# Unscaled k, a later third pair, and one-product maxima in the attention stage of a fused attention and expert kernel

## The chip, the cores and the metric

One core of a Trainium2 chip runs the whole program in one launch. The metric is the device time of one execution in microseconds (us). TensorE (PE) multiplies matrices into PSUM, VectorE (DVE) and ScalarE (ACT) read PSUM and SBUF, GpSimd (POOL) works on SBUF, SyncE (SP) issues the DMAs. Each engine takes its instructions in the order in which the program holds them, and waits on semaphores for the others.

## The reference

```python
def sm_attn(qq, kk, vv):                       # on q, k, v averaged over 4 neighbours
    s = scale * np.matmul(qq, kk.transpose(0, 1, 3, 2))
    a = np.exp(s - np.max(s, axis=-1, keepdims=True))
    a = a / (np.sum(a, axis=-1, keepdims=True) + 1e-09)
    return np.matmul(a, vv)
...
mask = np.abs(pos[:, None] - pos[None, :]) < factor        # factor = 4
scores = np.where(mask, scale * np.matmul(q, k.transpose(0, 1, 3, 2)), -1000000000.0)
...
return (out_up + out_local).astype(np.float32)  # pooled attention plus local attention

x = attention as [1152, 512]
x = (silu(x @ w_gate) * (x @ w_val)) @ w_out     # 512 -> 1536 -> 512
out = sum over 8 experts of P[:, e:e+1] * (relu(x @ w1[e]) @ w2[e])   # 512 -> 1024 -> 512
```

Shapes: q, k, v are (2, 8, 576, 64); `scale` is 1/8. P comes from a softmax of logits and 8 rounds of normalising rows and columns.

## The kernel before

The attention is worked in eight pairs of heads (pair 0 to 7; pairs 0 to 3 are the first batch). For each pair p these steps follow one another:

- `pooled` (L375): ACT multiplies k by -0.125 in place (L380), DVE sums q and k over four neighbours into `qd` and `kd` (L382, L383), ACT scales `kd` by 1/16 (L384). The two sums of pairs 2 and up are ordered behind the reciprocals of the pair before (`summed`).
- `scores` (L394): into three PSUM banks PE writes the mask (L399) and the local scores of five windows each (L402, banks 0 and 1), and the pooled scores (L405, bank 2). As k carries a minus sign, DVE takes minima: one reduction for each bank (L409 twice, L411), into the tile `stm`. ACT then does 13 exponentials with `scale=-1` and the minimum as bias (L417 ten times, L421 three times), each with a sum. DVE adds the sums (L425) and takes reciprocals (L426), POOL multiplies the exponentials by them (L428, L430).
- `turn` (L434): PE transposes the exponentials (L441, L445), ACT copies the result to SBUF as `at` (L447 to L450).
- `combine` (L453): PE multiplies with v (L463, L472), ACT and DVE form `x` (L475, L481), and `split` (L168, L169) makes an fp16 pair `xhl` of it.

`pooled_v` (L386) sums v over four neighbours on POOL. The banks of scores, transposes and outputs come from one ring of six (`bank`, tag `att`), so the scores of pair p+1 need banks that the exponentials of pair p still read. `attention` starts the scores of two pairs (`AHEAD`), then goes through turn(p), start(p+2), combine(p). `keep_warm` puts products of zeros into PE's queue for pairs 0 to 3, and `NWARM` such products stand at the very start.

Among this run the first steps of the next stage. For each of 12 slices f of `w_gate` and `w_val`: a load of float64 words (`load_gv`), the making of float32 from them on ACT and DVE (`from_f64`, L200 to L204: one ACT instruction and four of DVE), the maximum (L226 on ACT, then `allmax` over the partitions), and the fp16 split (`prep_gv`). `allmax` with `short` turns the column of maxima by a product (L159), reduces it (L160), and spreads the result by a second product (L161), which the users read from PSUM. The tile for this comes from `psg`, a ring of two banks that `keep_warm`, `vv` and the first products also use. `gv_step` then multiplies: 24 products of 512 columns for each f of batch 0, and 48 of 320 for each f of batch 1, which needs `xhl` of pairs 4 to 7. Slices 0, 1 and 2 of batch 0 are multiplied among pairs 4 to 7 (`EARLY`).

A scheduler that runs a model of the engines' times sets each engine's order within these rules (`gate` and `issue_after` add some).

Of the kernel before, what the change touches and what calls it, by code (L numbers as in the profile page):

```python
# [7 lines left out]
F32 = mybir.dt.float32  # L8
# [10 lines left out]
FAC, SD = 4, 144  # L19
# [9 lines left out]
WS = 64  # L29
WSTART = (0, 57, 114, 171, 228, 284, 341, 398, 455, 512)  # L30
WCUT = (0, 60, 117, 174, 231, 288, 344, 401, 458, 515, 576)
NW = 5
HQ = 48
# [16 lines left out]
UB = 8  # L50
KB = 5
HB = 4
NWARM = 5
NKEEP = 2
NQ = 3
V4B = 4
# [8 lines left out]
def tile_kernel(ctx, tc, qT, kT, vw, vd4, wgv, wo, wg2, w1, w2, out):  # L65
# [15 lines left out]
    def tmp(n, nm):  # L81
        return wp.tile([P, 16], F32, tag="tmp", bufs=56, name=nm)[:, :n]
# [15 lines left out]
    for n in range(32, P, 32):  # L98
# [7 lines left out]
    identb = ap.tile([P, P], BF16, tag="identb", bufs=1, name="identb")  # L106
    V.tensor_scalar(identb, dist, 0.0, None, op0=ALU.is_equal)
    maskb = ap.tile([P, NW, WS], BF16, tag="maskb", bufs=1, name="maskb")
    V.tensor_scalar(maskb, near[:, None, :].to_broadcast([P, NW, WS]), (2 * FAC - 1.0) ** 2, FAR,
                    op0=ALU.is_ge, op1=ALU.mult)  # L110
    ident = cp.tile([P, P], F32, name="ident")
    built.append(V.tensor_scalar(ident, dist, 0.0, None, op0=ALU.is_equal))
# [1 line left out]
    vdz = [ap.tile([HS, 2, P], F32, tag=f"vdz{i}", bufs=1, name=f"vdz{i}") for i in range(2)]  # L114
    stm = [ap.tile([P, 16], F32, tag=f"stm{i}", bufs=1, name=f"stm{i}") for i in range(2)]
    sts = [ap.tile([P, 16, 2], F32, tag=f"sts{i}", bufs=1, name=f"sts{i}") for i in range(2)]
    for i in range(2):
        V.memset(stm[i], 0.0)
        V.memset(sts[i][:, :, 0], 1.0)
        V.memset(sts[i][:, :, 1], 1e-9)  # L120
# [26 lines left out]
    def allmax(mx, n, nm, short=False):  # L147

        if n > 1:
            m = tmp(1, f"gm_{nm}")  # L150
            V.tensor_reduce(m, mx, axis=AX.X, op=ALU.max)  # L151
            mx = m
        if not short:
            g = tmp(1, f"g_{nm}")
            G.partition_all_reduce(g, mx, channels=P, reduce_op=RED.max)  # L155
            return g
        ps = psg.tile([P, 512], F32, tag="y", name=f"sm_{nm}")
        r = tmp(1, f"gr_{nm}")
        T.matmul(ps[:1, :P], lhsT=mx, rhs=ident, start=True, stop=True)  # L159
        V.tensor_reduce(r[:1], ps[:1, :P], axis=AX.X, op=ALU.max)  # L160
        T.matmul(ps[:, P:P + 1], lhsT=ones[:1], rhs=r[:1], start=True, stop=True)  # L161
        return ps[:, P:P + 1]

    def split(hi, lo, src, s, pool=False):
        if pool:
# [43 lines left out]
    def gate(after):  # L209
        return tc.issue_after(after.ins) if after else nullcontext()  # L210
# [156 lines left out]
    def attention():  # L367
# [7 lines left out]
        def pooled(pr):  # L375
            q, k = ld[pr]
            qd[pr] = ap.tile([P, SD, 2], F32, tag="qd", name=f"qd{pr}")
            kd[pr] = ap.tile([P, SD], F32, tag="kd", name=f"kd{pr}")
            with gate(exped.get(pr - 1) if pr > 1 else None):
                A.activation(k, k, AF.Copy, scale=-0.125)  # L380
            with gate(summed.get(pr - 1) if pr > 1 else None):
                V.tensor_reduce(kd[pr], k.rearrange("p (s a) -> p s a", a=FAC), axis=AX.X, op=ALU.add)  # L382
                V.tensor_reduce(qd[pr], q.rearrange("p (s a) j -> p s j a", a=FAC), axis=AX.X, op=ALU.add)  # L383
            A.activation(kd[pr], kd[pr], AF.Copy, scale=1.0 / (FAC * FAC))  # L384

        def pooled_v(pr):  # L386
            v4, vd = v4s[pr], vdz[pr % 2]
            vt = ap.tile([HS, 2, 2, P], F32, tag="vt", bufs=1, name=f"vt{pr}")
            with gate(scaled.get(pr - 1)):
                G.tensor_tensor(vt[:, 0], v4[:, :, 0], v4[:, :, 1], op=ALU.add)  # L390
                G.tensor_tensor(vt[:, 1], v4[:, :, 2], v4[:, :, 3], op=ALU.add)
                G.tensor_tensor(vd, vt[:, 0], vt[:, 1], op=ALU.add)

        def scores(pr):  # L394
            q, k = ld[pr]
            nm = f"{pr}"
            ps = bank(f"s{nm}", 3)
            for i in range(2):
                T.matmul(ps[i][:, :NW * WS], lhsT=identb, rhs=maskb.rearrange("p u w -> p (u w)"), start=True, stop=False)  # L399
                for c in range(NW):  # L400
                    ws = slice(WSTART[i * NW + c], WSTART[i * NW + c] + WS)
                    T.matmul(ps[i][:, c * WS:(c + 1) * WS], lhsT=q[:, ws].rearrange("p s j -> p (s j)"), rhs=k[:, ws],  # L402
                             start=False, stop=c == NW - 1)
            for t in range(NQB):
                T.matmul(ps[2][:2 * HQ, t * SD:(t + 1) * SD], lhsT=qd[pr][:, t * HQ:(t + 1) * HQ].rearrange("p s j -> p (s j)"),  # L405
                         rhs=kd[pr], start=True, stop=True)
            mx, sm = stm[pr % 2], sts[pr % 2]
            for i in range(2):
                V.tensor_reduce(mx[:, i:2 * NW:2], ps[i][:, :NW * WS].rearrange("p (u w) -> p u w", u=NW),  # L409
                                axis=AX.X, op=ALU.min)  # L410
            V.tensor_reduce(mx[:2 * HQ, 2 * NW:2 * NW + NQB], ps[2][:2 * HQ, :DW].rearrange("p (u w) -> p u w", u=NQB),  # L411
                            axis=AX.X, op=ALU.min)
            ex = ap.tile([P, DO + DW], F32, tag="ex", bufs=3, name=f"ex{nm}")
            for i in range(2):
                for c in range(NW):
                    w = 2 * c + i
                    A.activation(ex[:, w * WS:(w + 1) * WS], ps[i][:, c * WS:(c + 1) * WS], AF.Exp, scale=-1.0,  # L417
                                 bias=mx[:, w:w + 1], accum_out=sm[:, w, 0:1])
            for t in range(NQB):
                w = 2 * NW + t  # L420
                e = A.activation(ex[:2 * HQ, DO + t * SD:DO + (t + 1) * SD], ps[2][:2 * HQ, t * SD:(t + 1) * SD], AF.Exp,  # L421
                                 scale=-1.0, bias=mx[:2 * HQ, w:w + 1], accum_out=sm[:2 * HQ, w, 0:1])
            exped[pr] = e
            rs = ap.tile([P, 16], F32, tag="rs", name=f"rs{nm}")
            V.tensor_reduce(rs, sm, axis=AX.X, op=ALU.add)  # L425
            summed[pr] = V.reciprocal(rs, rs)  # L426
            x = ex[:, :DO].rearrange("p (w k) -> p w k", k=WS)
            G.tensor_tensor(x, x, rs[:, :2 * NW, None].to_broadcast([P, 2 * NW, WS]), op=ALU.mult)  # L428
            x = ex[:2 * HQ, DO:].rearrange("p (t k) -> p t k", t=NQB)
            scaled[pr] = G.tensor_tensor(x, x, rs[:2 * HQ, 2 * NW:2 * NW + NQB, None].to_broadcast([2 * HQ, NQB, SD]),  # L430
                                         op=ALU.mult)
            exs[pr] = ex

        def turn(pr):  # L434
            ex = exs[pr]
            nm = f"{pr}"
            pt = bank(f"t{nm}", 3)
            at = ap.tile([P, DO + 4 * SD], F32, tag="at", bufs=2, name=f"at{nm}")
            for c in range(NW):
                i, o = divmod(c * P, 512)  # L440
                T.transpose(pt[i][:, o:o + P], ex[:, c * P:(c + 1) * P], ident)  # L441
            for c in range(2):
                for t in range(NQB):
                    o = (1 - c) * P + t * 2 * HQ
                    turned[0] = T.transpose(pt[1 + c][:HS, o:o + 2 * HQ],  # L445
                                            ex[:2 * HQ, DO + t * SD + c * HS:DO + t * SD + (c + 1) * HS], ident[:2 * HQ, :2 * HQ])
            A.copy(at[:, :512], pt[0])  # L447
            A.copy(at[:, 512:DO], pt[1][:, :P])
            A.copy(at[:HS, DO:DO + 2 * SD], pt[1][:HS, P:P + 2 * SD])
            A.copy(at[:HS, DO + 2 * SD:], pt[2][:HS, :2 * SD])  # L450
            ats[pr] = at

        def combine(pr):  # L453
# [41 lines left out]
        def start(pr):  # L495
            if pr < NP:
                with tc.issue_after(built[0].ins), tc.issue_after(built[1].ins):
                    pooled(pr)
                scores(pr)
                if pr + NQ < NP:  # L500
                    load_pair(pr + NQ)

        for pr in range(AHEAD):
            start(pr)
            if pr == 0:
                pooled_v(0)
# [372 lines left out]
```

## Time and profile before

| | |
|---|---|
| time, median of 3 runs | 1024.42 us (1024.08 to 1025.7) |
| the profiled execution | 1024.88 us, span 1023.1 us |
| PE busy | 1006.8 us (98%) |
| DVE busy | 743.1 us (73%) |
| ACT busy | 444.5 us (43%) |
| POOL busy | 56.9 us (6%) |

The profiled execution's own time is 1.8 us above its span and 0.46 us above the median. Busy shares of the whole span are means over stages: the attention fills the first tenth of it. A busy PE may still be a slow or a half fed PE, since the ends of products are modelled; so the rows of single stretches are read below.

### The profile page before, as it was taken

The page shows a single profiled execution, that of the slowest core. Times are in us where ns is not written, and L with a number is a line of the kernel's source. Part 1 is how long each engine was busy: PE and PEld are TensorE (multiplying, and loading weights), DVE is VectorE, ACT ScalarE, POOL GpSimd, SP SyncE. Part 2 cuts the span into 40 slices and gives each one's busy share as a digit, 9 for nine tenths or more (in the row PEclk, how much of TensorE's full clock was granted, in tenths as well). Part 3 has the DMA queues.
Part 4 walks back from the last instruction along what each step waited for, and adds up shares of the span by engine and source line. Part 5 has one row for each costly group of instructions (what it writes and reads, how often), then busy time and mean ns, then how long its engine had stood idle before and what let it go on. Part 6 is the DMA issues. An engine that isn't in the chain of part 4 may idle for free.

```text
span 1023.1 us, 16441 instructions
## 1 busy us (share of the span) xinstructions
PE 1006.8 (98%) x6639; PEld 634.3 (62%) x6641; DVE 743.1 (73%) x1516; ACT 444.5 (43%) x926; POOL 56.9 (6%) x78
## 2 busy tenths in 40 slices
PE   8989999999999999999999999999999999999998
PEld 7765566565668657566566655756665575565644
DVE  5888788865937998797497669849757873974721
ACT  7986566665425555253235125314413521541300
POOL 4541000000001100000000000000000000000000
PEclk9989999999989999999999999999999999999999
DMA  9922143320010212121003012110301211020011
GB/s 291 277 102 97 42 165 128 121 83 1 21 63 1 84 52 73 42 81 44 5 38 122 3 42 83 43 33 9 125 1 42 83 42 42 1 83 1 1 42 52
DMA packets 12988, 67.92 MB, mean 66 GB/s; under 512 B 1584, under 2 KB 1840, under 8 KB 6512
## 3 DMA queue, kind: packets, MB, share of 16 engines
q1 hardware_dynamic: 12912, 66.87, 18.9%
q8 instruction: 52, 0.85, 0.3%
q14 instruction: 24, 0.20, 0.1%
HBM read 64.50 MB, written 2.36 MB: 65 GB/s over the span
## 4 chain that ended last, share of the span: by engine, by line
PE 77%; DVE 11%; ACT 6%; DMA 4%; issue 1%; SPq 0%; POOL 0%; ACTq 0%; DVEq 0%
PE y L176 34%; PE p L176 28%; PE gv L176 7%; PE wo L176 4%; DVE w L169 2%; DMA r<-in_w 2%; ACT ex L417 1%; DMA rawo<-in_wo 1%; DVE mxw L145 1%; DMA q<-in_qT 1%; DVE h L748 1%; PE s L402 1%; PE lgps L603 1%; DMA rawg<-in_wgv 1%; DVE cvg L203 1%
## 5 line engine op out<-in xcount | busy, mean ns | idle before, releaser
L176 PE MATMUL y<-w,hhl 128*128 128x512 f16 (+1 forms) x1752 | 396.2, 376 | 0.0
L176 PE MATMUL p<-bop,w 128*128 128x320 f16 (+1 forms) x2688 | 354.4, 286 | 1.7 <-DVE h L748 1.0
L176 PEld LDWEIGHTS <-w 128*128 128x128 f16 x2688 | 263.0, 98 | 91.8 <-issue 2.5
L176 PEld LDWEIGHTS <-hhl 128*128 128x128 f16 x1752 | 171.4, 98 | 178.2
L776 ACT ACTIVATE hhl<-h 128x640 f16<-128x640 f32 (+1 forms) x128 | 82.7, 676 | 161.6 <-DVE h L748 161.6
L176 PE MATMUL gv<-xhl,gv 128*128 128x320 f16 (+1 forms) x864 | 144.1, 328 | 1.9 <-DVE mv L357 0.8
L168 ACT ACTIVATE w<-r,s_w 128x256 f16<-128x256 f32 (+1 forms) x96 | 71.1, 783 | 117.4 <-PE y L176 86.3
L176 PEld LDWEIGHTS <-gv 128*128 128x128 f16 x864 | 84.6, 98 | 59.0 <-issue 5.6
L807 DVE SCALAR_TENSOR_TENSOR acc<-y,pe,acc 128x512 f32<-128x512 f32 (+1 forms) x64 | 47.3, 739 | 101.3 <-PE y L176 100.5
L777 DVE SCALAR_TENSOR_TENSOR hhl<-h,hhl 128x640 f16<-128x640 f32 (+1 forms) x128 | 94.1, 754 | 17.5 <-ACT hhl L776 16.6
L748 DVE SCALAR_TENSOR_TENSOR h<-p,u 128x256 f32<-128x256 f32 (+1 forms) x192 | 84.7, 453 | 15.7 <-PE p L176 9.8
L169 DVE SCALAR_TENSOR_TENSOR w<-r,s_w,w 128x256 f16<-128x256 f32 (+1 forms) x96 | 78.2, 833 | 16.8 <-ACT w L168 16.7
L176 PE MATMUL wo<-ahl,wo 128*128 128x320 f16 (+1 forms) x432 | 73.9, 333 | 0.0
L168 ACT ACTIVATE w<-cmb,s_w 128x512 f16<-128x512 f32 x64 | 43.0, 710 | 42.1 <-DVE cmb L280 40.0
L176 PEld LDWEIGHTS <-wo 128*128 128x128 f16 x432 | 43.3, 101 | 28.2
L748 DVE SCALAR_TENSOR_TENSOR u<-p,u 128x320 f32<-128x320 f32 (+1 forms) x128 | 57.4, 449 | 3.6 <-PE p L176 3.2
L765 ACT ACTIVATE s<-p 128x256 f32<-128x256 f32 (+1 forms) x64 | 25.4, 397 | 55.7 <-PE p L176 55.5
L145 DVE TENSOR_REDUCE mxw<-r 128x1 f32<-128x1024 f32 x32 | 37.4, 1213 | 16.3 <-DMA r<-in_w 16.1
L169 DVE SCALAR_TENSOR_TENSOR w<-cmb,s_w,w 128x512 f16<-128x512 f32 x64 | 46.1, 742 | 0.1
L300 ACT ACTIVATE j<-r 128x1024 f16<-128x1024 f32 x32 | 33.4, 1046 | 26.6 <-DMA r<-in_w 26.6
L155 POOL PARTITION_ALL_REDUCE g_w<-gm_w x16 | 6.3, 394 | 595.1 <-DVE gm_w L151 589.2
L748 DVE SCALAR_TENSOR_TENSOR u<-p,s 128x256 f32<-128x256 f32 (+1 forms) x64 | 28.8, 451 | 5.1 <-PE p L176 4.3
(192 smaller groups left out, 824.8 us busy)
## 6 DMA issues: line engine op xcount, KB each, us to landing
r<-in_w SPq DMA_DIRECT2D x32, 1024.0 KB, 4.8
rawg<-in_wgv SPq DMA_DIRECT2D x12, 1024.0 KB, 5.1
rawo<-in_wo SPq DMA_DIRECT2D x6, 1024.0 KB, 5.9
q<-in_qT SPq DMA_DIRECT2D x8, 576.0 KB, 6.9
vz<-in_vw SPq DMA_DIRECT2D x8, 320.0 KB, 6.7
k<-in_kT SPq DMA_DIRECT2D x8, 288.0 KB, 6.8
v<-in_vd SPq DMA_DIRECT2D x8, 288.0 KB
out<-acc SPq DMA_DIRECT2D x8, 256.0 KB, 2.0
```

The costliest lines, as they stand in the source:

```text
L145: V.tensor_reduce(o, i, axis=axis, op=ALU.max, apply_absolute_value=True)
L168: return (A.activation(hi, src, AF.Copy, scale=s), V.scalar_tensor_tensor(lo, src, s, hi, op0=ALU.mult, op1=ALU.subtract))
L169: V.scalar_tensor_tensor(lo, src, s, hi, op0=ALU.mult, op1=ALU.subtract))
L176: T.matmul(ps, lhsT=wf(i, k), rhs=xf(j, k), start=n == 0, stop=n == 3 * nk - 1)
L203: V.scalar_tensor_tensor(o, hi, 0xC0000000, o, op0=ALU.bitwise_and, op1=ALU.bitwise_or)
L300: A.activation(junk, t[:, 2 * j:2 * j + 2].rearrange("p a n -> p (a n)"), AF.Abs, accum_out=mx[:, 2 * i + j:2 * i + j + 1])
L402: T.matmul(ps[i][:, c * WS:(c + 1) * WS], lhsT=q[:, ws].rearrange("p s j -> p (s j)"), rhs=k[:, ws], start=False, stop=c == NW - 1)
L748: V.scalar_tensor_tensor(o, ps, HSC, u, op0=ALU.mult, op1=ALU.add)
L765: A.activation(s1, p1, AF.Copy, scale=HSC)
L776: ra = A.activation(t[:, 0], h, AF.Relu)
L777: rv = V.scalar_tensor_tensor(t[:, 1], h, 0.0, t[:, 0], op0=ALU.max, op1=ALU.subtract)
L807: V.scalar_tensor_tensor(acc[t][:, ds], ps, p[:, t:t + 1], acc[t][:, ds], op0=ALU.mult, op1=ALU.add)
```

## The change

In the diff the line numbers of before stand first. k and `kd` stay unscaled, so the scores keep their sign and lack the factor: the mask becomes negative, the reductions take maxima, a new DVE instruction multiplies the 16 columns of `stm` by a tile `fac` (-0.125 and -0.125/16), and the exponentials carry 0.125 and 0.125/16 as scale. Scores of pair 2 are started before the first turn, `pooled_v` comes behind the scaling of its own pair, the four copies of pair 0's transposes go to DVE, `allmax` with `short` does one product with the column spread over 128 as weights, and `NWARM` goes from 5 to 9.

```diff
-NWARM = 5
+NWARM = 9
...
-    V.tensor_scalar(maskb, near[:, None, :].to_broadcast([P, NW, WS]), (2 * FAC - 1.0) ** 2, FAR,
+    V.tensor_scalar(maskb, near[:, None, :].to_broadcast([P, NW, WS]), (2 * FAC - 1.0) ** 2, -FAR,
...
+    fac = ap.tile([P, 16], F32, tag="fac", bufs=1, name="fac")
+    V.memset(fac[:, :2 * NW], -0.125)
+    V.memset(fac[:, 2 * NW:], -0.125 / (FAC * FAC))
...
-        if not short:
-            g = tmp(1, f"g_{nm}")
+        g = tmp(1, f"g_{nm}")
+        if short:
+            ps = psg.tile([P, 512], F32, tag="y", name=f"sm_{nm}")[:, :P]
+            T.matmul(ps, lhsT=mx.to_broadcast([P, P]), rhs=ident, start=True, stop=True)
+            V.tensor_reduce(g, ps, axis=AX.X, op=ALU.max)
+        else:
             G.partition_all_reduce(g, mx, channels=P, reduce_op=RED.max)
-            return g
-        ps = psg.tile([P, 512], F32, tag="y", name=f"sm_{nm}")
-        r = tmp(1, f"gr_{nm}")
-        T.matmul(ps[:1, :P], lhsT=mx, rhs=ident, start=True, stop=True)
-        V.tensor_reduce(r[:1], ps[:1, :P], axis=AX.X, op=ALU.max)
-        T.matmul(ps[:, P:P + 1], lhsT=ones[:1], rhs=r[:1], start=True, stop=True)
-        return ps[:, P:P + 1]
+        return g
...
-            with gate(exped.get(pr - 1) if pr > 1 else None):
-                A.activation(k, k, AF.Copy, scale=-0.125)
...
-            A.activation(kd[pr], kd[pr], AF.Copy, scale=1.0 / (FAC * FAC))
...
-            with gate(scaled.get(pr - 1)):
+            with gate(scaled[pr]):
...
-                                axis=AX.X, op=ALU.min)
+                                axis=AX.X, op=ALU.max)
...
+            V.tensor_tensor(mx, mx, fac, op=ALU.mult)
...
-                    A.activation(ex[:, w * WS:(w + 1) * WS], ps[i][:, c * WS:(c + 1) * WS], AF.Exp, scale=-1.0,
+                    A.activation(ex[:, w * WS:(w + 1) * WS], ps[i][:, c * WS:(c + 1) * WS], AF.Exp, scale=0.125,
...
-            A.copy(at[:, :512], pt[0])
+            copy = A.copy if pr else V.tensor_copy
+            copy(at[:, :512], pt[0])
...
-        for pr in range(AHEAD):
+        for pr in range(AHEAD + 1):
...
-            start(pr + AHEAD)
+            if pr:
+                start(pr + AHEAD)
```

The order on DVE at the very start, around the first reductions of pairs 0 and 1 (`s0_1` is bank 1 of pair 0's scores, `rs` the sums and reciprocals). Before:

```order
L382 TENSOR_REDUCE kd1_211<-k1_135 128x144
L383 TENSOR_REDUCE qd1_210<-q1_137 128x288
L409 TENSOR_REDUCE stm0_111<-s0_0_156 128x5
L409 TENSOR_REDUCE stm0_111<-s0_1_157 128x5
L411 TENSOR_REDUCE stm0_111<-s0_2_158 96x3
L425 TENSOR_REDUCE rs0_191<-sts0_113 128x16
L426 RECIPROCAL rs0_191<-rs0_191 128x16
L409 TENSOR_REDUCE stm1_112<-s1_0_216 128x5
```

Now:

```order
L382 TENSOR_REDUCE qd1_216<-q1_144 128x288
L407 TENSOR_REDUCE stm0_115<-s0_1_162 128x5
L409 TENSOR_REDUCE stm0_115<-s0_2_163 96x3
L407 TENSOR_REDUCE stm1_116<-s1_0_220 128x5
L411 TENSOR_TENSOR stm0_115<-stm0_115,fac_119 128x16
L407 TENSOR_REDUCE stm1_116<-s1_1_221 128x5
L409 TENSOR_REDUCE stm1_116<-s1_2_222 96x3
L411 TENSOR_TENSOR stm1_116<-stm1_116,fac_119 128x16
```

The multiplication by `fac`, which every exponential of pair 0 reads, stands behind all three reductions of pair 0 and behind the first of pair 1.

The order on DVE ahead of the exponentials of pair 4, with the float32 words of slice 1 (`cvg1`) and the rounding tiles of slice 0 (`u_gv0`, `s_gv0`, `i_gv0`) among it. Before:

```order
L383 TENSOR_REDUCE qd4_622<-q4_258 128x288
L382 TENSOR_REDUCE kd4_623<-k4_256 128x144
L481 TENSOR_TENSOR x11_549<-o1_0_521,avd1_547 128x288
L481 TENSOR_TENSOR x11_549<-o1_1_522,avd1_547 128x224
L481 TENSOR_TENSOR tail_121<-o1_1_522,avd1_547 128x64
L409 TENSOR_REDUCE stm0_111<-s4_0_628 128x5
L169 SCALAR_TENSOR_TENSOR xhl_127<-x10_417,s_x10_383,xhl_127 128x512
L409 TENSOR_REDUCE stm0_111<-s4_1_629 128x5
L169 SCALAR_TENSOR_TENSOR xhl_127<-x11_549,s_x10_383,xhl_127 128x512
```

Now, the last rows of the same stretch:

```order
L407 TENSOR_REDUCE stm0_115<-s4_1_628 128x5
L203 TENSOR_SCALAR cvg1_582<-cvg1_582 128x1024
L142 TENSOR_SCALAR u_gv0_573<-u_gv0_573 128x1
L204 SCALAR_TENSOR_TENSOR cvg1_582<-rawg1_445,cvg1_582 128x1024
L143 TENSOR_SCALAR s_gv0_574<-u_gv0_573 128x1
L144 TENSOR_SCALAR i_gv0_575<-u_gv0_573 128x1
L409 TENSOR_REDUCE stm0_115<-s4_2_629 96x3
L205 SCALAR_TENSOR_TENSOR cvg1_582<-rawg1_445,cvg1_582 128x1024
L541 TENSOR_SCALAR iv0_0_1029<-i_gv0_575,i_x10_387 128x1
L411 TENSOR_TENSOR stm0_115<-stm0_115,fac_119 128x16
```

Before, five rows stood between the reciprocal of pair 3 and the first reduction of pair 4, after which five of its exponentials could start; now nineteen rows stand between that reciprocal and the multiplication by `fac`, which all thirteen wait for.

## Rows read from the trace of the kernel before

**Rows 1.** Windows: start:end, length, busy of PE, PEld, DVE, ACT, POOL, clock, DMA, GB/s.

```profile
40.00:60.00 20.00, 19.41 (x233) 15.53 (x231) 18.39 (x38) 18.80 (x77) 6.80 (x9) 1.00 0.65 207
70.00:80.00 10.00, 9.22 (x53) 5.19 (x53) 8.51 (x25) 6.58 (x29) 3.37 (x4) 0.50 0.00 1
82.92:98.10 15.18, 14.70 (x149) 8.31 (x148) 12.66 (x29) 10.38 (x21) 0.38 (x1) 1.00 0.36 108
```

**Rows 2.** PE's longest wait from 109 us on: sum, count, mean.

```profile
PE lgps L603 <- ACT x L618: 1.5, 1, 1.5
```

**Rows 3.** Timeline of the start: start, duration, engine, line, operation, tiles, [idle before].

```profile
1.17 2.31 PE L90 MATMUL pw<-warm 128*128 128x512 bf16 x5 [1.17 <-DVE dist L93]
5.82 4.51 PE L402 MATMUL s<-k,q 128*128 128x64 f32 x20
10.76 0.31 ACT L417 ACTIVATE ex<-s,stm 128x64 f32<-128x64 f32 x1 [2.43 <-DVE stm L409]
20.99 2.44 PE L402 MATMUL s<-k,q 128*128 128x64 f32 x20 [0.87 <-ACT k L380]
```

**Rows 4.** Timeline, single places on DVE, ACT and PE.

```profile
20.14 0.25 DVE L426 RECIPROCAL rs<-rs 128x16 f32<-128x16 f32 x1
36.90 0.25 DVE L426 RECIPROCAL rs<-rs 128x16 f32<-128x16 f32 x1
38.93 0.74 DVE L481 TENSOR_TENSOR x<-o,avd 128x288 f32<-128x288 f32 x2
39.60 0.21 DVE L481 TENSOR_TENSOR tail<-o,avd 128x64 f32<-128x64 f32 x1
41.92 0.35 ACT L417 ACTIVATE ex<-s,stm 128x64 f32<-128x64 f32 x1
47.54 0.24 DVE L426 RECIPROCAL rs<-rs 128x16 f32<-128x16 f32 x1
79.11 0.23 DVE L426 RECIPROCAL rs<-rs 128x16 f32<-128x16 f32 x1
108.88 3.71 PE L176 MATMUL gv<-xhl,gv 128*128 128x320 f16 x26
```

**Rows 5.** Groups of instructions, 20 to 80 us: busy, mean ns of one, idle before.

```profile
L383 DVE TENSOR_REDUCE qd<-q 128x288 f32<-128x1152 f32 x6 | 7.8, 1295 | 0.0
L409 DVE TENSOR_REDUCE stm<-s 128x5 f32<-128x320 f32 x12 | 5.7, 483 | 0.8 <-PE s L402 0.6
L203 DVE SCALAR_TENSOR_TENSOR cvg<-rawg,cvg 128x1024 uint32<-128x1024 uint32 x4 | 5.3, 1318 | 0.0
L382 DVE TENSOR_REDUCE kd<-k 128x144 f32<-128x576 f32 x6 | 4.4, 738 | 0.0
L380 ACT ACTIVATE k<-k 128x576 f32<-128x576 f32 x6 | 4.3, 718 | 0.0
L169 DVE SCALAR_TENSOR_TENSOR xhl<-x,s_x,xhl 128x512 f16<-128x512 f32 x4 | 3.9, 987 | 0.5 <-ACT xhl L168 0.5
L447 ACT COPY at<-t 128x512 f32<-128x512 f32 x6 | 3.7, 616 | 0.0
L411 DVE TENSOR_REDUCE stm<-s 96x3 f32<-96x432 f32 x6 | 3.6, 595 | 0.3 <-PE s L405 0.3
L201 DVE TENSOR_SCALAR cvg<-cvg 128x1024 f32<-128x1024 f32 x4 | 2.7, 686 | 1.8 <-ACT cvg L200 1.8
L138 DVE TENSOR_SCALAR u_gv<-sm_gv 128x1 f32<-128x1 f32 x2 | 0.3, 153 | 0.0
```

**Rows 6.** Chain of waits, steps in order of time: start, duration.

```profile
10.76 3.07 ACT ex L417 x20
13.83 1.05 ACT ex L421 x6
76.29 4.65 PE gv L176 x12
94.75 2.69 PE gv L176 x12
```

More of the change, by code (lines that the diff above doesn't have):

```diff
@@ L409, in scores @@
                 V.tensor_reduce(mx[:, i:2 * NW:2], ps[i][:, :NW * WS].rearrange("p (u w) -> p u w", u=NW),
-                                axis=AX.X, op=ALU.min)
+                                axis=AX.X, op=ALU.max)
             V.tensor_reduce(mx[:2 * HQ, 2 * NW:2 * NW + NQB], ps[2][:2 * HQ, :DW].rearrange("p (u w) -> p u w", u=NQB),
-                            axis=AX.X, op=ALU.min)
+                            axis=AX.X, op=ALU.max)
+            V.tensor_tensor(mx, mx, fac, op=ALU.mult)
             ex = ap.tile([P, DO + DW], F32, tag="ex", bufs=3, name=f"ex{nm}")
@@ L421, in scores @@
                 e = A.activation(ex[:2 * HQ, DO + t * SD:DO + (t + 1) * SD], ps[2][:2 * HQ, t * SD:(t + 1) * SD], AF.Exp,
-                                 scale=-1.0, bias=mx[:2 * HQ, w:w + 1], accum_out=sm[:2 * HQ, w, 0:1])
+                                 scale=0.125 / (FAC * FAC), bias=mx[:2 * HQ, w:w + 1], accum_out=sm[:2 * HQ, w, 0:1])
             exped[pr] = e
@@ L446, in turn @@
                                             ex[:2 * HQ, DO + t * SD + c * HS:DO + t * SD + (c + 1) * HS], ident[:2 * HQ, :2 * HQ])
-            A.copy(at[:, :512], pt[0])
-            A.copy(at[:, 512:DO], pt[1][:, :P])
-            A.copy(at[:HS, DO:DO + 2 * SD], pt[1][:HS, P:P + 2 * SD])
-            A.copy(at[:HS, DO + 2 * SD:], pt[2][:HS, :2 * SD])
+            copy = A.copy if pr else V.tensor_copy
+            copy(at[:, :512], pt[0])
+            copy(at[:, 512:DO], pt[1][:, :P])
+            copy(at[:HS, DO:DO + 2 * SD], pt[1][:HS, P:P + 2 * SD])
+            copy(at[:HS, DO + 2 * SD:], pt[2][:HS, :2 * SD])
             ats[pr] = at
```

## The prediction, made before the changed kernel ran

> **What bounds the kernel now.** I read the windows first, and stage by stage, since the mean of the whole span (PE 98%) hides the attention. In 40 to 60 us DVE is busy for 18.39 of 20 us and ACT for 18.80 [rows 1]: both are full, and they are full because each does the other work of the stage while the other one is at the softmax. PE's 19.41 us there is not work at full rate. From the first products of batch 1 on (`gv` of 320 columns, at 108.88 us [rows 4]) PE is dense: the waits for other engines have 1.5 us as their longest [rows 2]. PE's order behind that product is as good as the same in both kernels. So the question is one: when does the first 320-column product start? What comes later moves with it. It needs `xhl` of pairs 4 to 7, and these hang on a chain that I follow by the reciprocals of each pair: they start at 20.14 (pair 1), 36.90 (pair 3), 47.54 (pair 4) and 79.11 us (pair 7) [rows 4].
>
> **The change part by part.**
>
> *The barrier.* This is the part that decides. Before, the first five exponentials of a pair wait for one reduction; the others follow as the second and third reductions come. Now all 13 wait for the multiplication by `fac`, which waits for three reductions, and it stands in DVE's one queue behind whatever was put between them. The multiplication itself is small: between 0.15 us (a 128x1 step) and 0.25 us (the 128x16 reciprocal) [rows 5, 4]; I take 0.15. The reciprocal of a pair in its turn waits for all the exponentials, so DVE can't go on with the next pair. Thus a pair now costs a sum of two parts: DVE's work from a reciprocal to the next `fac`, and ACT's exponentials.
>
> Pair 4 worked out, as its order is shown above. Before, from the reciprocal at 36.90 to the first exponential at 41.92 us it took 5.0 us, and 5.6 us more to the next reciprocal [rows 4]. Now nineteen instructions stand between: three of `x1` (0.74 + 0.21), `kd` 0.74, `qd` 1.30, three reductions (2 x 0.48 + 0.60), `xhl` 0.99, two conversions of 0.69 and two of 1.32, `g_gv0` (between 0.15 and 0.60; 0.25), five small ones of 0.15 [rows 4, 5]: 10.5 us. Single instructions overlap by some 0.07 us at their borders (38.93 + 0.74 = 39.67 stands beside a next start at 39.60 [rows 4]), 1.4 us for twenty. With `fac` that is 9.3 us, and 0.9 us more for the reciprocal's own end and for a wait on ACT's conversion that precedes these: 10.2 us. Then 13 exponentials, 4.1 us (3.07 + 1.05 [rows 6]), with one conversion of slice 2 on ACT put between them (as long as L226, 1.1 us [rows 5]), and behind them on DVE the sum, three instructions of `x2`, a conversion of 1.32 and the reciprocal: 7.9 us in all. The link takes 18.1 us where it took 10.6.
>
> The other links by the same durations and the changed order. Reciprocal 1 to exponentials 2: `kd`, `qd`, the third reduction, `fac`, and the pooled scores between, 3.5; to reciprocal 2, 4.6. To exponentials 3: 9.0, since all four DVE steps that make slice 0, `x0` and `g_v0` stand in front; to reciprocal 3, 6.3 (two other ACT steps lie among the exponentials). Pair 5: 5.9 + 4.6, no conversion in front. Pair 6: 9.4 + 5.0 (`x3`, its `xhl`, slice 3). Pair 7: 8.7 + 4.6. From reciprocal 1 to reciprocal 7 that is 3.5 + 4.6 + 9.0 + 6.3 + 10.2 + 7.9 + 5.9 + 4.6 + 9.4 + 5.0 + 8.7 + 4.6 = 79.7 us, against 79.11 - 20.14 = 59.0 us before [rows 4]: 20.7 us more.
>
> *The start.* `NWARM` adds four products to five that took 2.31 us [rows 3]; they end ahead of the data of pair 0, so they cost nothing. [...] In return the exponentials of pair 0 wait for three reductions and one of pair 1: start 12.3 us instead of 10.76 [rows 6]. Pair 1 follows at 16.4, and reciprocal 1 comes to end at 21.0 where it was 20.4: 0.6 us later. Pair 2's scores ahead of the first transposes cost 2.4 us of PE's time there [rows 3], under the exponentials of pair 1.
>
> *k unscaled.* Eight multiplications of 0.72 us go from ACT [rows 5], and those of `kd`. In 40 to 60 us ACT was full [rows 1], so this would be worth something if the two engines still overlapped. As ACT now waits at each pair for `fac`, it is worth nothing on the chain: DVE sums k directly, and stands later anyway.
>
> *Four copies to DVE (pair 0).* The nearest rows are ACT's copy of 512 columns, 0.62 us, and DVE's reduction of 432 columns from PSUM, 0.60 us [rows 5]. So the four take some 1.6 to 2.0 us on either engine; on DVE they lie under the exponentials of pair 2, which run on ACT. I take 0, and 2.0 if `fac` of pair 2 were late. [...]
>
> *Pooled v behind the scaling, one-product maxima.* POOL is busy for 6.80 of 20 us [rows 1]; its queue has room, and pooled v is needed only after the copies of the same pair: 0, at most 0.5 us a pair. The maximum loses a one-column product of PE and its wait; DVE reduces 128 rows of 128 in place of one row. Between -0.3 and +0.3 us for each of some 14; I take 0, since neither is last on the chain in the early slices.
>
> *The tail.* Some of the 20.7 us is paid back. Before, 108.88 - 79.34 = 29.5 us lie between the end of reciprocal 7 and the first 320-column product [rows 4]. There PE was held up: in 70 to 80 us its granted clock was 0.50 [rows 1], twelve products of 512 columns took 4.65 us at 76.29 and 2.69 later [rows 6]. Now, as the exponentials of pair 7 are later, two of these groups of twelve have been done by then. Left for PE are, by the changed order, 60 products of 512 columns (2.69/12 = 0.224 us each [rows 6], 13.4 us) and the transposes of pair 7 and outputs of pairs 6 and 7. For these: in 82.92 to 98.10 us PE was busy for 14.70 us [rows 1] with just these and with 36 such products (8.1 us) and two small ones (some 0.8); 5.8 us remain. Reciprocal 7 ends at 21.0 + 79.7 = 100.7; 1.7 us go by until the copies of pair 6, which stand behind the exponentials of pair 7 on ACT, are done; 100.7 + 1.7 + 13.4 + 5.8 = 121.6 us. That is 12.7 us after 108.88.
>
> **Sum.** 0.6 + 20.7 - 8.6 in the tail = 12.7 us. The profiled execution took 1024.88 us (0.46 above the median of 1024.42), so 1037.6 us, rounded to 1037.5.
>
> **The rivals.** *A*, the forecast: the chain through `fac` with a warm start, 1037.5. If single links are 0.5 us off each way, its own range is 1031 to 1043.
>
> [...]
>
> *C: ScalarE was the bound (the other side).* ACT is the fuller engine [rows 1]. If DVE's conversions find room under the exponentials and `fac` comes just behind the third reduction, what decides is ACT's work, and eight multiplications of 0.72 us are gone: 1024.9 - 5.8 = 1019 us. It decides once the steps of DVE between a reciprocal and the next `fac` sum to less than the 5.0 us of before; in pair 5 they nearly do (5.9), in pairs 3, 4, 6 and 7 they are at 8.7 to 10.2. [...]
>
> *D: it cancels.* The chain slips as in A, but by some 10 us only, and PE, which has to do the same products in any case, loses none of them: 1025, within 0.2% (about 2 us, what a measurement of this kernel can tell from no change).
>
> *E:* the chain slips and half of the slip is paid back beyond the tail as well: 1029, slower but below A's range.
>
> **How the numbers follow.** A 0.52, B 0.25, C 0.11, D 0.07, E 0.05. Faster is C, 0.11; the same is D, 0.07; slower is A, B and E, 0.82. The range goes from 1026 (C and D left out, 0.18) to 1045 (B and the upper ends of its unknowns, 2 us for the copies and 0.5 us for POOL): 1026 to 1045.
>
> **What would show it.** In the trace after: the first exponential of a pair starts right behind a 128x16 multiplication on DVE (right), not behind a reduction. The reciprocals of pairs 3, 4 and 7 near 44, 62 and 100 us (A), 49, 67 and 105 (B), or at or ahead of 36.9, 47.5 and 79.1 (C). ACT idle before the exponentials, by 3 us and more in pairs 3, 4, 6 and 7 (A); PE's twenty score products of pair 0 near 2.4 us (A) or 4.5 us (B). The first product of 320 columns near 121.6 us; waits of PE behind it as short as before. I am wrong if that product comes late and the end doesn't (then PE had slack behind it), or if DVE shows that its steps overlap more than I allow.

## The result

| | before | changed |
|---|---|---|
| time, median | 1025.06 us (4 runs, 1024.08 to 1027.13) | 1039.71 us (4 runs, 1037.35 to 1043.07) |
| ratio of the times | | 1.0143, 95% interval 1.0108 to 1.0177 |
| the profiled execution, its span | 1024.88, 1023.1 us | 1038.61, 1036.8 us |
| reciprocal of pair 1, 3, 4, 7 starts | 20.14, 36.90, 47.54, 79.11 us | 19.73, 44.36, 63.31, 101.47 us |
| first product of batch 1 (320 columns) | 108.88 us | 124.3 us |

The kernel became slower by 1.4%, inside the range and on the side that was forecast. The forecast of 1037.5 us lies 1.1 us under the profiled execution and 2.2 under the median. Of the runs told below, one execution each of e7 and e12 took over 1.5% longer than the fastest of its kernel, and the ratios and medians leave both out.

The profile of the changed kernel, windows with the columns of [rows 1]. The first two windows are one link of the chain: from the reciprocal of pair 3 to the multiplication by `fac` of pair 4, and from there to the reciprocal of pair 4.

```profile
44.36:54.08 9.72, 6.43 (x84) 5.00 (x82) 9.72 (x20) 3.88 (x7) 4.56 (x5) 0.99 0.46 159
54.08:63.31 9.23, 5.76 (x24) 4.33 (x25) 5.98 (x13) 8.30 (x35) 0.00 (x0) 0.50 0.43 149
40.00:60.00 20.00, 11.78 (x111) 8.29 (x109) 13.36 (x27) 14.11 (x57) 4.56 (x5) 0.85 0.57 193
```

In the first window DVE never stops (9.72 of 9.72 us) and ACT has 3.88 us to do; in the second ACT has 8.30 of 9.23 and DVE waits in part. Over 40 to 60 us both engines fall from 18.39 and 18.80 us [rows 1] to 13.36 and 14.11: they take turns. PE, busy for 5.76 of 9.23 us, shows a granted clock of 0.50 in the second window.

The same link as a timeline (start, duration, engine, line, operation, [idle before]) on DVE and ACT, as the forecast worked it out:

```profile
44.36 0.25 DVE L425 RECIPROCAL rs<-rs 128x16 f32<-128x16 f32 x1
47.19 0.48 DVE L407 TENSOR_REDUCE stm<-s 128x5 f32<-128x320 f32 x1
...
52.31 0.60 DVE L409 TENSOR_REDUCE stm<-s 96x3 f32<-96x432 f32 x1
52.83 1.21 DVE L205 SCALAR_TENSOR_TENSOR cvg<-rawg,cvg 128x1024 uint32<-128x1024 uint32 x1
53.96 0.20 DVE L541 TENSOR_SCALAR iv<-i_gv,i_x 128x1 f32<-128x1 f32 x1
54.08 0.17 DVE L411 TENSOR_TENSOR stm<-stm,fac 128x16 f32<-128x16 f32 x1
52.37 1.15 ACT L169 ACTIVATE gv<-cvg,s_gv 128x1024 f16<-128x1024 f32 x1 [5.28 <-DVE s_gv L143]
54.13 1.06 ACT L227 ACTIVATE rawg<-cvg 128x1024 f16<-128x1024 f32 x1 [0.61 <-DVE cvg L205]
55.19 0.29 ACT L416 ACTIVATE ex<-s,stm 128x64 f32<-128x64 f32 x1
63.31 0.25 DVE L425 RECIPROCAL rs<-rs 128x16 f32<-128x16 f32 x1
```

The first reduction of pair 4 is over at 47.7 us, and in the kernel before five exponentials could have followed it. Here they start at 55.19 us, with `fac` at 54.08. ACT had stood idle for 5.28 us ahead of 52.37. The last step ahead of these exponentials is not `fac` itself but ACT's own maximum over slice 1 (L227, to 55.19 us), whose words DVE made ahead of `fac`: the conversions stand ahead of the exponentials in both queues.

The waits of DVE in 9 to 110 us (us in total, times, longest), first the kernel before, then the changed one:

```profile
DVE rs L425 <- ACT ex L421: 8.3, 5, 2.4
```

```profile
DVE rs L424 <- ACT ex L420: 15.1, 6, 4.1
```

It is the other half of the turn: DVE waits for the exponentials almost twice as long. The end of the stage, from the list of one line's instructions up to the first 320-column product (count, ns, first and last start, forms):

```profile
L177 PE MATMUL gv<-xhl,gv x97: 296/379/634, 82.4 to 124.3; 128*128 128x512 f16 x96, 128*128 128x320 f16 x1
```

As before, 96 products of 512 columns come ahead of it; it starts 15.4 us later. Behind it PE's waits are as they were (the longest again 1.5 us, as in [rows 2]), and 912.5 us follow where 914.2 followed before.

### The profile page after: what moved, and what is told of

The parts are those of the page before. It is cut to its first block, busy times and chain, and to the rows that moved or that the text cites. A ratio compares the mean times of both kernels' runs of the same rounds, so it can differ in the third digit from the quotient of the medians.

```text
span 1036.8 us, 16426 instructions
## 1 busy us (share of the span) xinstructions
PE 1008.8 (97%) x6629; PEld 636.3 (61%) x6631; DVE 748.8 (72%) x1530; ACT 437.5 (42%) x906; POOL 58.3 (6%) x78
## 4 chain that ended last, share of the span: by engine, by line
PE 82%; DVE 10%; ACT 5%; DMA 1%; issue 1%; SPq 0%; ACTq 0%; DVEq 0%
PE y L177 36%; PE p L177 31%; PE gv L177 9%; PE wo L177 4%; ACT ex L416 2%; DVE cvg L204 1%; DVE cvg L205 1%; DMA rawo<-in_wo 1%; DVE qd L382 1%; DVE w L170 1%; PE lgps L604 1%; DMA q<-in_qT 1%; ACT ex L420 1%; DVE cvg L203 1%; DVE xhl L170 1%
## 5 line engine op out<-in xcount | busy, mean ns | idle before, releaser
L778 DVE SCALAR_TENSOR_TENSOR hhl<-h,hhl 128x640 f16<-128x640 f32 (+1 forms) x128 | 94.2, 752 | 16.6 <-ACT hhl L777 15.4
L749 DVE SCALAR_TENSOR_TENSOR h<-p,u 128x256 f32<-128x256 f32 (+1 forms) x192 | 84.8, 451 | 18.4 <-PE p L177 12.7
```

The lines of the kernel that those rows point to most:

```text
L749: V.scalar_tensor_tensor(o, ps, HSC, u, op0=ALU.mult, op1=ALU.add)
L778: rv = V.scalar_tensor_tensor(t[:, 1], h, 0.0, t[:, 0], op0=ALU.max, op1=ALU.subtract)
```

## The experiments

The theory: all 13 exponentials of a pair wait for one DVE instruction, which the scheduler puts behind other DVE work; so DVE and ACT take turns. Its rivals: other parts of the change make the loss, or the wait itself costs as much wherever it stands. Each experiment stands with its ratio to the kernel before, timed beside it. In all of them a scheduler sets the order anew, so an edit moves other instructions too; where that matters it is said.

| | ratio, 95% interval | median us | reciprocal 1, 3, 7 | first 320-column product |
|---|---|---|---|---|
| changed kernel | 1.0143, 1.0108 to 1.0177 | 1039.71 | 19.7, 44.4, 101.5 | 124.3 |
| e1 barrier on before | 1.0225, 1.0188 to 1.0262 | 1048.3 | 23.3, 53.3, 110.6 | 136.8 |
| e2 fac per bank | 1.0020, 0.9999 to 1.0040 | 1027.3 | 19.1, 41.3, 89.1 | 116.5 |
| e3 conversions behind fac | 1.0036, 1.0010 to 1.0061 | 1028.43 | 19.6, 43.8, 94.7 | 115.1 |
| e4 k scaled again | 0.9994, 0.9973 to 1.0014 | 1024.73 | 17.3, 40.0, 84.8 | 109.2 |
| e5 five warm products | 1.0151, 1.0116 to 1.0186 | 1040.02 | 23.1, 47.5, 104.6 | 128.0 |
| e6 before, nine warm products | 1.0013, 0.9985 to 1.0041 | 1024.85 | 17.2, 42.9, 85.9 | 116.6 |
| e7 per bank and behind | 0.9964, 0.9944 to 0.9984 | 1020.67 | 19.0, 42.0, 89.6 | 109.1 |
| e8 k scaled and behind | 1.0022, 1.0001 to 1.0042 | 1027.87 | 17.0, 41.4, 81.3 | 113.4 |
| e9 e7 with k multiplied | 1.0065, 1.0041 to 1.0089 | 1031.51 | 18.9, 44.9, 96.3 | 121.7 |
| e10 e7, third pair late | 1.0051, 1.0033 to 1.0069 | 1030.11 | 19.3, 46.6, 97.4 | 119.2 |
| e11 e7, copies on ACT | 1.0031, 1.0015 to 1.0047 | 1028.61 | 18.7, 42.8, 90.2 | 113.2 |
| e12 e7, two-product maxima | 1.0068, 1.0039 to 1.0096 | 1031.3 | 19.6, 42.2, 86.8 | 115.3 |

**The barrier alone, on the kernel before.**

```diff
+    fac = ap.tile([P, 16], F32, tag="fac", bufs=1, name="fac")
+    V.memset(fac, 1.0)
...
+            V.tensor_tensor(mx, mx, fac, op=ALU.mult)
```

> The kernel before (k still scaled, minima), with one DVE instruction more for each pair: the 16 minima are multiplied by a tile of ones, and all 13 exponentials wait for that. It computes the same. Theory (the wait of all exponentials for one instruction behind the conversions on DVE makes the loss): the reciprocals come late as in the changed kernel, reciprocal 3 at 43 to 46 us, 4 at 62 to 66, 7 at 98 to 106 us, and the time is 1035 to 1043 us. Rival (unscaled k, the copies on DVE, or pair 2's early scores make the loss): the multiplication costs its own 0.16 us per pair, reciprocal 7 stays within 3 us of 79, and the time is 1024 to 1027 us.

It was 2.25% slower, 5 us above what the theory expected, and its reciprocals came 4 to 7 us later than the theory had them. The link of pair 4, timeline of DVE and ACT:

```profile
53.33 0.25 DVE L429 RECIPROCAL rs<-rs 128x16 f32<-128x16 f32 x1
...
62.79 0.47 DVE L411 TENSOR_REDUCE stm<-s 128x5 f32<-128x320 f32 x1
63.19 0.59 DVE L413 TENSOR_REDUCE stm<-s 96x3 f32<-96x432 f32 x1
63.99 0.69 DVE L203 TENSOR_SCALAR cvg<-cvg 128x1024 f32<-128x1024 f32 x1 [0.21 <-ACT cvg L202]
64.60 0.70 DVE L415 TENSOR_TENSOR stm<-stm,fac 128x16 f32<-128x16 f32 x1
65.42 0.32 ACT L420 ACTIVATE ex<-s,stm 128x64 f32<-128x64 f32 x1 [1.46 <-DVE stm L415]
69.85 0.25 DVE L429 RECIPROCAL rs<-rs 128x16 f32<-128x16 f32 x1
```

From reciprocal to exponentials it takes 12.1 us, with four conversions, the split of slice 0 and the first step of slice 2 ahead of the product with ones. One multiplication by 1 in each pair is enough for the whole loss. It is more than enough: the changed kernel, which has the other parts too, is 0.8% faster than e1.

**The barrier split in three.**

```diff
             for i in range(2):
-                V.tensor_reduce(mx[:, i:2 * NW:2], ...)
+                m = mx[:, i:2 * NW:2]
+                V.tensor_reduce(m, ...)
+                V.tensor_tensor(m, m, fac[:, i:2 * NW:2], op=ALU.mult)
...
-            V.tensor_tensor(mx, mx, fac, op=ALU.mult)
```

> The changed kernel, with fac multiplied bank by bank: three small DVE instructions, each right behind its reduction as far as the scheduler has it so, in place of one behind all three. Theory: the first five exponentials of a pair start again ahead of the conversions; reciprocal 7 comes at 84 to 93 us and the time falls to 1026 to 1033 us, in spite of 16 DVE instructions more. Rival (the loss lies in other parts of the change): 1037 to 1041 us, and reciprocal 7 near 101 us.

16 DVE instructions more, and 1.2% less time than the changed kernel: back within 0.2% of the kernel before, though not shown to be equal to it. Reciprocal 7 came at 89.1 us, in the middle of what was expected. In pair 4 the exponentials of the first bank start behind the first small product (45.87 us, with 45.17 for the product), and in 40 to 60 us DVE is busy for 18.90 us and ACT for 16.55, where they had 13.36 and 14.11 in the changed kernel and 18.39 and 18.80 before [rows 1]:

```profile
45.17 0.58 DVE L409 TENSOR_TENSOR stm<-stm,fac 128x5 f32<-128x5 f32 x1
45.87 0.32 ACT L417 ACTIVATE ex<-s,stm 128x64 f32<-128x64 f32 x1
40.00:60.00 20.00, 17.59 (x189) 12.93 (x189) 18.90 (x43) 16.55 (x60) 10.30 (x10) 1.00 0.62 196
```

**The barrier left, the work ahead of it moved behind.** Each slice is converted one pair later, and its DVE steps are queued behind `fac`.

```diff
-CONV = {1: (1, 2), 3: (3,), 5: (4,), 7: (5,)}
+CONV = {1: (0,), 2: (1,), 3: (2,), 4: (3,), 5: (4,), 7: (5,)}
...
-            V.tensor_tensor(mx, mx, fac, op=ALU.mult)
+            facd[pr] = V.tensor_tensor(mx, mx, fac, op=ALU.mult)
...
-            with gate(exped[3] if f == 1 else None):
-                conv_gv(f, x1_done[pr])
+            with gate(facd.get(pr + 2)):
+                conv_gv(f, exped[2] if f == 0 else x1_done[pr - 1])
```

> The changed kernel, with the four DVE steps that make slices 0 to 4 ordered behind the multiplication by fac of the next pair (they are called one pair later and queued behind it); the barrier itself stays. Theory (the price is the DVE work that stands between a reciprocal and fac, not the wait as such): the links from reciprocal to fac fall to 5 to 7 us, the conversions lie under the exponentials, reciprocal 7 comes at 80 to 88 us, and the time is 1021 to 1029 us. Rival (a wait of all 13 for one instruction costs whatever stands ahead of it): reciprocal 7 at 96 us or later and 1034 us or more.

The time fell to 1028.43 us, as the theory had it; reciprocal 7 came at 94.7, between the two expectations. The windows of the link of pair 4, reciprocal to `fac` and `fac` to reciprocal:

```profile
43.76:48.95 5.19, 5.13 (x51) 4.26 (x49) 5.19 (x12) 2.74 (x7) 4.56 (x5) 1.00 0.35 98
48.95:54.72 5.77, 3.44 (x47) 2.35 (x47) 5.47 (x13) 5.48 (x29) 0.00 (x0) 0.96 0.95 337
```

The link is 10.96 us in place of 18.95, as long as the 10.64 of the kernel before [rows 4], and in its second half DVE and ACT are both busy (5.47 and 5.48 of 5.77 us). So the wait as such is cheap; what stands ahead of it is dear. Not all links healed: the one from reciprocal 2 to reciprocal 3 kept 14.7 us, as the conversion of slice 1 on ACT stands ahead of `avd` in ACT's queue and waits for its load (slice 0 was converted at 29.75 us).

```profile
33.54 1.13 ACT L201 ACTIVATE cvg<-rawg 128x1024 f32<-128x1024 f32 x1 [2.63 <-DMA rawg<-in_wgv]
34.88 0.76 DVE L482 TENSOR_TENSOR x<-o,avd 128x288 f32<-128x288 f32 x2 [3.45 <-ACT avd L476]
```

**k scaled again, no fac.**

```diff
+            with gate(exped.get(pr - 1) if pr > 1 else None):
+                A.activation(k, k, AF.Copy, scale=-0.125)
...
+            A.activation(kd[pr], kd[pr], AF.Copy, scale=1.0 / (FAC * FAC))
...
-            V.tensor_tensor(mx, mx, fac, op=ALU.mult)
```

(with minima, a positive mask and `scale=-1.0` again)

> The changed kernel, with k scaled again on ACT, minima and no fac; the later third pair's order, pooled v, the copies, the one-product maxima and nine warm products stay. Theory: no barrier, so reciprocal 7 returns to 74 to 80 us and the time to 1020 to 1027 us. Rival (the other parts share the loss): 1031 us or more.

The time is that of the kernel before (0.9994). Of the expectation the time held and reciprocal 7 did not: it came at 84.8 us, 5.7 later than before, and still the first 320-column product starts at 109.2. So an earlier chain isn't the only thing that sets this product: PE's 96 products ahead of it must be done too.

**Five and nine warm products.**

```diff
-NWARM = 9
+NWARM = 5
```

> The changed kernel with five products of zeros at the start in place of nine; from pair 2 on DVE's order is the same. Theory (the nine products bring the higher clock for the first scores): the twenty score products of pair 0 take about 4.5 us again, reciprocal 1 comes at 22.5 to 24 us in place of 19.7, all later reciprocals slip by as much, and the time is 1040 to 1045 us. Rival (the clock would have risen without them): reciprocal 1 at 19 to 21 us and 1036 to 1040 us.

> The kernel before with nine products of zeros at the start and nothing else. Theory: reciprocal 1 at 17 to 18 us in place of 20.1, the later ones earlier by 1 to 3 us, the time 1021 to 1024 us. Rival (what the start gains is lost in the tail, where PE has its products of 512 columns to do in any case): 1024 to 1027 us.

PE's first score products in the changed kernel and, below, in the same kernel with five:

```profile
1.17 4.02 PE L90 MATMUL pw<-warm 128*128 128x512 bf16 x9 [1.17 <-DVE dist L93]
5.56 1.52 PE L400 MATMUL s<-k,q 128*128 128x64 f32 x10
7.06 1.23 PE L400 MATMUL s<-k,q 128*128 128x64 f32 x10
```

```profile
1.17 2.31 PE L90 MATMUL pw<-warm 128*128 128x512 bf16 x5 [1.17 <-DVE dist L93]
5.55 2.23 PE L400 MATMUL s<-k,q 128*128 128x64 f32 x10
7.85 2.23 PE L400 MATMUL s<-k,q 128*128 128x64 f32 x10
```

With five, ten products take 2.23 us; with nine the first ten take 1.52 and the second ten 1.23. The granted clock has a mean of 1.00 over 0 to 20 us in both, so it does not show what makes the difference. The reciprocals slip by 3.3 us at pair 1 and 3.2 at pair 7, and the first 320-column product by 3.6, as expected. The times don't show it (1.0151 and 1.0143, with intervals of 0.35% each way): the 909.9 us behind that product were 2.6 less than in the changed kernel's profile. On the kernel before, the nine products bring reciprocal 1 forward by 2.9 us and the time not at all (1.0013): the time is the rival's. That the gain is lost in the tail isn't shown: the profile belongs to one of the longer executions (1033.25 us, 8 above the median), and there reciprocal 3 is already 6 us later than before.

**Both repairs.**

> The changed kernel with both repairs: fac bank by bank, and the conversions of slices 0 to 4 behind the last of these. Theory (two parts of one loss): reciprocal 7 at 80 to 88 us, the time 1021 to 1026 us, less than with either repair alone (1027.3 and 1028.4). Rival (both repairs give back the same microseconds, or the tail eats the rest): 1026 to 1030 us.

(the edits of e2 and e3 together, with the conversions behind the last of the three products with `fac`)

1020.67 us, by the ratio 0.36% less than the kernel before, interval 0.16 to 0.56%: the time is less than with either repair alone, as the theory had it, and this version beats both kernels. Reciprocal 7 is not the reason, at 89.6 us against the 80 to 88 expected. In its profile the first 320-column product starts at 109.1 us, as in the kernel before, and the 5 us between the two profiled executions lie behind it (914.2 us there in the kernel before, 908.9 here); some three of them are told below, under the hardware.

**Which parts of the change are worth something, once the barrier is mended.** The same repair without `fac`, and then e7 with one part undone at a time.

In e8 the third reduction takes the place of `fac` in the ordering:

```diff
-            V.tensor_reduce(mx[:2 * HQ, 2 * NW:2 * NW + NQB], ...)
+            facd[pr] = V.tensor_reduce(mx[:2 * HQ, 2 * NW:2 * NW + NQB], ...)
```

> The changed kernel with k scaled again, minima and no fac, and with the conversions of slices 0 to 4 ordered behind the third reduction of the next pair. Theory: reciprocal 7 at 76 to 84 us and 1019 to 1024 us. Rival (ACT, which scales k again, is now as full as in the kernel before, so nothing is left to gain): 1024 to 1028 us.

```diff
+            with gate(exped.get(pr - 1) if pr > 1 else None):
+                A.activation(k, k, AF.Copy, scale=1.0)
...
+            A.activation(kd[pr], kd[pr], AF.Copy, scale=1.0)
```

> The kernel of e7 (fac bank by bank, conversions behind), with ACT's two multiplications per pair put back, by a factor of 1: k and kd pass through ACT as in the kernel before, and the rest computes as in e7. Theory (once DVE and ACT overlap again, ACT's 0.72 us for k in each of eight pairs stands on the path, the mechanism of the rival that was to make the change faster): 1024 to 1029 us, 4 to 7 us above e7. Rival (k's scaling hides even there): 1020 to 1023 us.

```diff
-        for pr in range(AHEAD + 1):
+        for pr in range(AHEAD):
...
-            if pr:
-                start(pr + AHEAD)
+            start(pr + AHEAD)
```

> The kernel of e7 with the scores of pair 2 behind the first turn again, as in the kernel before. In e7 PE waits 6.2 us at 15 to 21 us for qd of pair 2, with the first transposes behind that in its queue. Theory (the early third pair blocks PE's queue more than it helps): the transposes of pair 0 start near 16 us in place of 22.8, reciprocal 3 comes 1 to 3 us earlier than 42.0, and the time falls to 1017 to 1021 us. Rival (PE has slack there, and pair 2 loses its head start): reciprocal 2 comes 1 to 3 us later than 25.7 and the time is 1021 to 1025 us.

```diff
-            copy = A.copy if pr else V.tensor_copy
+            copy = A.copy
```

> The kernel of e7 with the four copies of pair 0's transposes on ACT again. Theory (the copies cost the same on either engine and lie beside a wait): no change, 1019 to 1023 us. Rival (VectorE is the slower reader of PSUM and the fuller engine): 1016 to 1019 us. Other rival (ACT is late with the exponentials of pair 2): 1023 to 1026 us.

In e12 `allmax` is again, word for word, what the minus lines of the change show.

> The kernel of e7 with the maximum over partitions made by two products again (a column turned, its maximum, a second product that spreads it). Theory (the prediction's: neither form is last on the chain): 1019 to 1024 us. Rival (the second product and its way from DVE back to PE and to DVE delay the fp16 slices, so that the products of 512 columns start later): 1024 to 1029 us.

The amounts here and below are differences of the ratios, times 1025 us, each good to some 3 us. e8's time is its rival's: 5.9 us above e7 and no better than before. e9 put the two multiplications alone back and cost 10.4 us against e7, more than the 4 to 7 expected; ACT spends 8.2 us on them (5.6 for k, 2.6 for `kd`). So the mechanism of the rival that was to make the change faster is there: k's scaling does stand on the path, once DVE and ACT overlap. PE shows one place of it, the scores of pair 2, which wait for k, as that multiplication is ordered behind the exponentials of pair 1 (in e7 these scores start at 12.4 us, and reciprocal 2 comes 2.9 us earlier):

```profile
19.26 4.53 PE L404 MATMUL s<-k,q 128*128 128x64 f32 x20 [5.32 <-ACT k L382]
```

e10's theory fell. (The title and e4's text speak of a later third pair; the change starts the scores of pair 2 earlier, and e10 puts them back.) In e7 (and in the changed kernel) PE's queue does stand for 6.16 us with the pooled scores of pair 2 at its head, and without that the transposes of pair 0 start at 16.40 us, as expected. But the time rose by 8.9 us, beyond the rival's range too, reciprocal 2 came 2.4 us later and reciprocal 3 4.6 us later: pair 2's head start is worth more than the wait. First the row of the changed kernel, then of e10:

```profile
21.99 1.72 PE L403 MATMUL s<-kd,qd 128*96 128x144 f32 x6 [6.16 <-DVE qd L382]
```

```profile
16.40 1.33 PE L442 MATMUL t<-ident,ex 128*128 128x128 f32 x5 [4.04 <-POOL ex L429]
```

e11 (6.9 us above e7) fits none of its three expectations: its time lies above them all, though what the first rival starts from is in the traces (DVE's copy of 512 columns took 0.68 us and ACT's 0.60 in the changed kernel, and DVE was busy for 20.00 us in 40 to 60 us of e7, ACT for 14.47), and ACT isn't late with pair 2 (reciprocal 2 at 25.56 us, in e7 at 25.70). Where its loss comes from is open. e12 (10.7 us above) went its rival's way, and beyond its range. Reciprocal 7 comes 2.8 us earlier than in e7 and the first 320-column product 6.2 us later. At the first group of 512 columns 5.8 of these are there already (79.66 us, in e7 73.84): the scores of pair 7 stand ahead of it, and PE's granted clock has a mean of 0.78 over 60 to 80 us (0.83 in e7). The second product of a maximum is seen to hold PE up only later, where it waits for DVE, and the group behind it takes 4.44 us for 12 products, where the groups at 85.82 and 91.78 us take 2.76; the mean granted clock is 0.93 over 80 to 100 us and 0.95 over 100 to 120 (1.00 in e7 for both). So the rival's mechanism is there, but most of the delay isn't shown to be its work:

```profile
97.30 0.38 PE L164 MATMUL sm_gv<-gr_gv,ones 1*128 1x1 f32 x2 [0.46 <-DVE gr_gv L163]
98.26 4.44 PE L179 MATMUL gv<-xhl,gv 128*128 128x512 f16 x12 [0.58 <-DVE act L568]
```

The four amounts (10.4, 8.9, 6.9 and 10.7 us) can't be added: together they are 37 us, and the kernel before, which lacks all four parts, is 4 us slower than e7. Each edit lets the scheduler set a new order, and how much of an amount is the part and how much the order was not separated.

## Why the prediction was right, and which of its terms were off

- **The barrier** is right as the cause, shown by e1 (alone, it makes the loss) and by e2 and e3 (split, or with the work behind it, most of the loss goes). Of the signs set down for it, the exponentials start within 0.15 us of the end of `fac` in pairs 0, 2, 3 and 6, and 0.5 to 0.9 us after it in pairs 4, 5 and 7, where another step stands ahead of them in ACT's queue. ACT is idle for 5.9 to 7.1 us between reciprocal and exponentials in pairs 3, 4 and 6, but for 1.8 us only in pair 7, where 3 and more were forecast.
- **The link of pair 4** was worked out as 10.2 + 7.9 us and measured 10.6 + 8.4 (reciprocal end at 44.61, exponentials at 55.19, reciprocal end at 63.56).
- **The chain** from reciprocal 1 to 7 was 79.7 us by the forecast and measured 101.47 - 19.73 = 81.7. The term most off is the link of pair 2, 3.5 us to its exponentials: it took 4.9. PE's granted clock fell to 0.50 (20 to 26 us) in its wait of 6.16 us for `qd`, and the pooled scores took 1.72 us there (0.93 in pair 0, at a clock of 1.00).
- **The start** came 1.0 us earlier than forecast (reciprocal 1 ends at 19.98, not 21.0): the exponentials of pair 0 start at 11.35 us, not 12.3. That the first scores come faster with nine products was the author's estimate, and the 0.6 us of the sum rests on it. No run shows a change of the clock behind it: in the kernel before, the granted clock is 1.00 both where twenty score products took 4.51 us (5.82 to 10.33) and where they took 2.44 (20.99 to 23.43). What the runs show is the time of the products: 1.52 and 1.23 us for the two tens of pair 0 with nine, 2.23 each with five. Rival B, by which they keep the 4.51 us of before and the time is 1042, is out.
- **The tail** was 20.9 us by the forecast and took 22.6 (124.33 - 101.72). One group of twelve 512-column products took 4.09 us at a granted clock of 0.67 (the next one 2.76 us at 1.00), which no term had, and PE waited 0.84 us more:

```profile
105.85 4.09 PE L177 MATMUL gv<-xhl,gv 128*128 128x512 f16 x12
110.60 2.76 PE L177 MATMUL gv<-xhl,gv 128*128 128x512 f16 x12
114.20 0.47 PE L463 MATMUL o<-at,vdz 72*64 72x144 f32 x4 [0.84 <-issue]
```

- **The sum**: -1.0 + 2.0 + 1.7 = 2.7 us too little up to the first 320-column product, and 1.7 us less behind it: 1038.6 where 1037.5 was forecast. Good agreement of the sum, in part by terms that cancel. Rivals D and E are out: the slip is 22.4 us at reciprocal 7, 15.4 at that product and 13.7 at the end of the profiled executions.
- **Reciprocal 7 as the measure** holds only where it is late. In the profiles that have it at 94 us or later the product follows it by 20 to 26 us; where it comes at 79 to 90 us the product starts at 108.9 to 116.6, in no order (89.6 and 109.1 in e7, 81.3 and 113.4 in e8).
- **The terms put at nothing** are where the working was weakest. e1 without them is 8.6 us slower than the changed kernel with them. Two differences are seen in the rows: the start (reciprocal 1 at 23.3 in e1, 3.6 later), whose faster score products the forecast did count, and the link of pair 2 (reciprocal 1 to 2 takes 13.2 us in e1 and 9.5 in the changed kernel), which fits the early third pair, charged with PE's time only. What unscaled k is worth beside an undivided `fac` was put at nothing too, and no run shows it alone. The sum held since it was made from the changed order, where the early pair's link is short, and not by adding parts to the old chain.
- **The four copies**: the one of 512 columns took 0.68 us on DVE where ACT takes 0.60:

```profile
24.64 0.68 DVE L447 COPY at<-t 128x512 f32<-128x512 f32 x1
45.11 0.60 ACT L447 COPY at<-t 128x512 f32<-128x512 f32 x1
```

  Yet e11, which has these copies on ACT, was slower than e7: the 0.08 us are not what decides there.
- **Rival C** had the right mechanism and the wrong condition. By e9 ACT's scaling of k does cost once the engines overlap; in the changed kernel they don't. Its point of decision, DVE's work between a reciprocal and `fac` against 5.0 us, fits: with 5.2 us in e3's link that link was as short as before. An exponential with a scale of 0.125 starts 0.29 us behind the one before it (55.19, then 55.48 us), as with the scale of -1 before (41.92, then 42.21 us).

## What to carry to other kernels

An instruction that gathers several results before the next engine may start costs more than its own time: it can cost all that a scheduler or an order puts ahead of it on its engine (here `fac` took 0.17 us in pair 4, and the link 18.95 us in place of 10.64). Where one engine's saving puts such a join into the loop of two engines that are both full, split the join along the parts that the other engine takes, and queue movable work behind it; here only the version with both was faster than the kernel before. To price such a change, walk the two engines' new order link by link; a price for each part, added to the old chain, would have missed here by some 8 us (e1 against the changed kernel).

## What the runs showed of the hardware

PE waits once for 1.5 us near 285 us, in the kernel before [rows 2] as in e7 (and at 301 us in the changed one). In the profiled execution of before the granted clock then falls in 289 to 309 us; in that of e7, with the same wait, it doesn't. Windows as in [rows 1], first before, then e7:

```profile
269.00:289.00 20.00, 18.50 (x136) 13.35 (x135) 19.55 (x37) 13.19 (x23) 0.44 (x1) 0.98 0.28 106
289.00:309.00 20.00, 20.00 (x132) 14.69 (x130) 2.18 (x5) 0.80 (x1) 0.00 (x0) 0.84 0.00 1
```

```profile
269.00:289.00 20.00, 18.50 (x141) 13.57 (x138) 18.88 (x36) 12.52 (x22) 0.43 (x1) 1.00 0.28 106
289.00:309.00 20.00, 20.00 (x155) 15.02 (x155) 2.51 (x5) 1.25 (x2) 0.00 (x0) 1.00 0.00 1
```

With a clock of 0.84 PE did 132 products in 20 us, with 1.00 it did 155, so the fall costs some 3 us. Between these two executions it explains over half of the difference behind the first 320-column product (914.2 us in before, 908.9 in e7). As far as one profile of each kernel shows, e7's edits don't decide it: over the 100 us that hold the same wait the mean clock is 1.00 in e1 and e2 as in e7, 0.97 in the kernel before, the changed kernel and e4, and 0.95 in e6. And in e1, the kernel before with one instruction more in each pair, 908.7 us follow the first 320-column product, as few as in e7. So where e7's 0.36% comes from stays open: the lowest times of the two kernels in the same runs, 1019.24 and 1021.07 us, still differ by some 2 us.
